# Attention moves shared between the GpSimd and SyncE queues in a fused attention and two-MLP kernel

## The chip, the cores and the metric

The kernel runs on one core of one Trainium2 chip. The metric is the device time of one execution in microseconds (us). Most executions of a kernel agree within 0.3%. The engines of the core are TensorE (PE in the profile, its weight loads PEld), VectorE (DVE), ScalarE (ACT), GpSimd (POOL) and SyncE (SP), which computes nothing and issues transfers. A name with a q (SPq, ACTq) is that engine's queue of issued instructions; transfers run on the core's 16 DMA engines.

## The reference

All tensors are float32. Attention has 4 batches, 12 heads, 448 rows and a head dimension of 64; the 12 heads' scores are mixed with one 12x12 matrix ahead of the softmax and with another behind it. Two MLPs follow, on 1792 tokens of 768 features.

```python
scores = scale * np.matmul(q, k.transpose(0, 1, 3, 2))
scores = np.einsum('bhij,hg->bgij', scores, w_pre)
scores = scores - np.max(scores, axis=-1, keepdims=True)
attn = np.exp(scores)
attn = attn / (np.sum(attn, axis=-1, keepdims=True) + 1e-09)
attn = np.einsum('bhij,hg->bgij', attn, w_post)
x = np.matmul(attn, v)            # -> [1792, 768], heads side by side
h = (x @ w1) * (x @ w2) @ w3 @ w_out
h = h @ w_in
out = np.maximum(0.01 * h, h) @ w_out2
```

## The kernel before, in words

The first 310 us or so are attention, the rest the MLPs. The change concerns attention alone, and there its beginning.

The 448 query rows of a batch are cut into four chunks (three of 120 rows, one of 88, which is computed with 90). The order of chunks (`order`) begins with the short one. A chunk consists of blocks of 10 query rows; two blocks are a group, and the program walks over groups two at a time (the loop over `k`, which grows by 2; each turn is called a step here, so k = 24 is the thirteenth step).

For a chunk, `qk` computes the scores of one head pair p in one go: two matmuls into PSUM (tile `pq`, for the even head e = 0 and the odd head e = 1), then a copy of each into SBUF (tile `s`, 120 rows x 2 heads x 448), by ScalarE or VectorE. The mixing over heads needs the heads of one query row on the partition axis. That is what `move` does: a DMA takes one head's 120 x 448 scores from tile `s` and writes them to ten partitions, twelve apart, of a row tile `sr`. A chunk has six pairs, so twelve moves. There are three row tiles (`rows_of`, numbered 0, 1, 2, each 128 x 12 x 448), used in turn; all three are cleared once at the beginning, in `constants_load`, since some partitions are never written.

`premix` multiplies a row tile with the pre-mixing matrix (`pm` in PSUM, from `sr` and `kpre` alone); `tops` takes row maxima on VectorE (`mx`); `softmax` exponentiates on ScalarE (tile `e`, sums in `sm`); `weigh` scales by the reciprocal of the sums, three of four tiles on GpSimd and the fourth on VectorE; `postmix` multiplies with the post-mixing matrix (`po`) on TensorE, and VectorE transposes the result (`ap`); `av` multiplies with v (`px`), and ScalarE writes `y`, with one subtraction on GpSimd. The first premix of a row tile needs all twelve moves of the chunk.

The work is issued in an order that is written out by hand (no scheduler moves it within attention). `qk` runs ahead: LEAD = 10 groups' pairs, eleven pairs in all, are computed before the first step with `early=True`, and each step then makes the pairs of two more groups (three at k = 16 and k = 20, by AT). In a step come: the `qk` matmuls, loads of q and k for later steps by SyncE, `tops`, `softmax`, `evict` (the copies of the new pairs and their moves), `av`, `weigh`, `postmix` of the step before, and the premixes of the next step. `turn(n)` are n matmuls without a result that fill time on TensorE.

The queues before: moves go by SyncE's queue, in the order in which the program reaches them, between the loads of q, k and v and the stores of y. Only the even heads of the first chunk go by ScalarE's queue. GpSimd's queue has no transfer in it. At the beginning VectorE clears row tile 0, and GpSimd clears `kpre`, `kpost` and row tiles 1 and 2. In the early `qk` VectorE copies the odd heads, and of the first chunk both heads of every second pair; ScalarE copies the rest.

Of the kernel before, what the change touches and what calls it, by code (L numbers as in the profile page):

```python
# [11 lines left out]
ACTF = mybir.ActivationFunctionType  # L12
# [10 lines left out]
def attention_moe_kernel(ctx: ExitStack, tc, qt, kt, vt, w_pre, w_post, w1, w2, w3t, w_out, w_in2, w_out2, out):  # L23
# [7 lines left out]
    nc = tc.nc  # L31
# [7 lines left out]
    P = 128  # L39
    JP = 112  # L40
    NJ = S // JP
    IB = 10
    LEAD, AT, SKIP = 10, (16, 20), 4
    CH = qt.shape[-1]
    TERMS = ((0, 0), (0, 1), (1, 0))
    scale = 1.0 / float(D) ** 0.5
# [71 lines left out]
    def attention(seam):  # L118
        with ExitStack() as es, ExitStack() as left:
# [30 lines left out]
            def constants_load():  # L150
                nc.vector.memset(rows_of[0], 0.0)
                for t in (kpre, kpost):
                    nc.gpsimd.memset(t, 0.0)
                for i in (1, 2):
                    nc.gpsimd.memset(rows_of[i], 0.0)
                for n, w in enumerate((w_pre, w_post)):
                    nc.sync.dma_start(out=wrep[:, n, :], in_=w)

# [68 lines left out]
            def qk(b, c, p, early=False):  # L227
# [28 lines left out]

                def out():
                    for e in range(2):
                        if early and (e or (b, c) == order[0] and p % 2):
                            nc.vector.tensor_copy(t[:m, e, :], pq[e][:m])  # L260
                        else:
                            nc.scalar.activation(out=t[:m, e, :], in_=pq[e][:m], func=ACTF.Copy)  # L262
                    for e in range(2):
                        args = srt[b, c], t[:m, e, :], 2 * p + e
                        move(*args, nc.sync if e or (b, c) != order[0] else nc.scalar)

                evs.append(out)
                if early:
# [4 lines left out]
                w = t.shape[0] // IB  # L273
                ends["sync"] = queue.dma_start(out=dst[SKIP + h:SKIP + h + H * (IB - 1) + 1:H, :w, :], in_=t)

            evs, staged = [], []

            def evict():
                while evs:
# [217 lines left out]
            for k in range(0, NG + 2, 2):  # L497
# [7 lines left out]
                old = [n for g in done for n in groups[g]]  # L505
                before = ets.pop(k - 2, None)
                ahead = [x for g in made[k] for x in slot(g)]
                for x in ahead:
                    qk(*x)
                for job in (k_load, q_load):  # L510
# [13 lines left out]
                if drain:  # L524
                    if old:
                        turns = postmix(old, before, now=False)
                        turn_out(turns.pop(0))
                    if k > LAST:
                        next(seam, None)
                    if now:  # L530
                        weigh(fresh, sm, ets[k], True)
                    while turns:
                        turn_out(turns.pop(0))
                else:
                    weigh(fresh, sm, ets[k], False)
                while lows:
                    lows.pop(0)()
                if old and not drain:
# [583 lines left out]
```

## Time and profile before

| | |
|---|---|
| three runs, us | 1218.69, 1223.53, 3006.95 (median 1223.53) |
| the profiled execution's own time, us | 1220.24 |
| its span in the profile, us | 1218.5 |
| granted TensorE clock, mean | 0.997 |
| busy: TensorE / weight loads | 98% / 81% |
| busy: VectorE / ScalarE / GpSimd | 73% / 45% / 17% |
| DMA, mean over the span | 162 GB/s |

The span is the time from the first to the last instruction of the profiled execution, and its own time is a little longer. Busy shares are means over stages with different limits: GpSimd is busy almost only in the first 310 us. Rows of the trace name a line of the kernel, the engine, the operation and the tiles (written <- read). A bracket at the end of a row of a timeline holds how long the engine was idle before it and what ended that idle time, by the profile's inference; a wait for several things is put down to the one that came last by it. A granted clock of 1.00 is 2.4 GHz, one of 0.50 is 1.2 GHz.

### The profile page before, as it was taken

The numbers are of one execution on the slowest core, as the hardware profiler recorded it, in microseconds if no ns is written. First come the engines' busy times: TensorE is split into PE (matmuls) and PEld (weight loads), VectorE is DVE, ScalarE is ACT, GpSimd is POOL, SyncE is SP. The second block draws the span as 40 slices with busy tenths as digits, with TensorE's granted clock in tenths as the row PEclk, the third lists the DMA queues.
The fourth block names the chain that finished last, engine by engine and source line by source line (L and its number), as shares of the span: only waits on it lengthen the run. The fifth ranks groups of instructions, "written<-read, shape, count | busy, mean of one in ns | idle before, by whom it ended". The sixth has DMA issues, their size and how long they took to land.

```text
span 1218.5 us, 22377 instructions
## 1 busy us (share of the span) xinstructions
PE 1197.1 (98%) x8782; PEld 985.3 (81%) x8782; DVE 885.8 (73%) x1538; ACT 550.8 (45%) x1120; POOL 206.8 (17%) x160
## 2 busy tenths in 40 slices
PE   8899999999999999999999999999999999999998
PEld 5245555554478999998899999999999999999998
DVE  6677887888889998547795867667776657376572
ACT  3677777766755454323454342352233433322120
POOL 4566767666310000000000000000000000000000
PEclk9999999999999999999999999999999999999999
DMA  6876776756957756489674636063242221212012
GB/s 212 222 201 192 211 231 183 221 168 184 300 160 256 238 187 198 162 275 352 221 238 145 216 96 208 26 221 115 92 129 70 65 70 52 72 33 72 26 53 91
DMA packets 134282, 196.81 MB, mean 162 GB/s; under 512 B 26304, under 2 KB 114976, under 8 KB 134176
## 3 DMA queue, kind: packets, MB, share of 16 engines
q1 hardware_dynamic: 129656, 192.77, 49.7%
q10 hardware_dynamic: 4520, 2.61, 0.7%
q8 instruction: 69, 1.13, 0.4%
q14 instruction: 37, 0.30, 0.1%
HBM read 114.57 MB, written 42.07 MB: 129 GB/s over the span
## 4 chain that ended last, share of the span: by engine, by line
PE 82%; DVE 8%; DMA 5%; ACT 3%; issue 1%; ACTq 0%; SPq 0%; POOL 0%; DVEq 0%; POOLq 0%
PE pm L587 29%; PE po L601 19%; PE pp L898 17%; DVE ap L375 6%; PE pw L659 6%; PE px L392 5%; PE po L360 3%; ACT e L323 3%; DMA sr<-s 3%; PE pq L248 2%; DVE mx L316 1%; DMA x<-scr 1%; PE pm L306 1%; DMA q<-in_q_dram 1%; PE turn L293 1%
## 5 line engine op out<-in xcount | busy, mean ns | idle before, releaser
L587 PE MATMUL pm<-x,ws 128*128 128x384 f32 (+1 forms) x1152 | 233.9, 364 | 0.0
L587 PEld LDWEIGHTS pm<-x,ws 128*128 128x128 f32 x1152 | 208.7, 188 | 24.5 <-issue 0.6
L339 POOL TENSOR_SCALAR e<-e,sm 128x448 f32<-128x448 f32 x126 | 181.9, 1456 | 141.0 <-DVE sm L333 123.1
L323 ACT ACTIVATE e<-pm,mx 128x448 f32<-128x448 f32 x180 | 111.7, 632 | 85.3 <-DVE mx L316 80.8
L375 DVE STREAM_TRANSPOSE ap<-po 128x512 f32<-128x512 f32 (+3 forms) x228 | 116.7, 571 | 25.2 <-PE po L360 24.5
L898 PE MATMUL pp<-t,w 128*128 128x448 f32 x576 | 124.5, 368 | 0.0
L601 PE MATMUL po<-ws,g 128*128 128x384 f32 x672 | 117.2, 334 | 0.0
L601 PE MATMUL po<-wo,g 128*128 128x384 f32 x672 | 117.1, 334 | 0.0
L898 PEld LDWEIGHTS pp<-t,w 128*128 128x128 f32 x576 | 108.1, 188 | 10.9
L601 PEld LDWEIGHTS po<-wo,g 128*128 128x128 f32 x672 | 116.6, 188 | 0.2
L601 PEld LDWEIGHTS po<-ws,g 128*128 128x128 f32 x672 | 116.6, 188 | 0.0
L316 DVE TENSOR_REDUCE mx<-pm 128x1 f32<-128x448 f32 x180 | 98.5, 603 | 11.7 <-PE pm L306 11.7
L100 ACT ACTIVATE wc<-wr 128x768 f32<-128x768 f32 (+1 forms) x72 | 61.6, 858 | 85.0 <-DMA wr<-in_moe_w_dram 29.1
L392 PEld LDWEIGHTS px<-ap,vs 96*64 96x64 f32 (+1 forms) x1536 | 77.7, 136 | 22.1 <-ACT e L323 16.7
L898 PE MATMUL pp<-b,w 128*128 128x448 f32 x432 | 95.5, 368 | 0.0
L608 DVE TENSOR_TENSOR acc<-po,acc 128x384 f32<-128x384 f32 x84 | 45.5, 555 | 66.5 <-PE po L601 66.4
L306 PE MATMUL pm<-sr,kpre 64*64 64x448 f32 x720 | 82.0, 555 | 9.0 <-DMA sr<-s 4.8
L392 PE MATMUL px<-ap,vs 96*64 96x120 f32 (+3 forms) x1536 | 87.6, 266 | 2.9 <-ACT e L323 1.0
L360 PE MATMUL po<-e,kpost 64*32 64x512 f32 (+1 forms) x1472 | 89.1, 586 | 0.8 <-POOL e L339 0.7
L262 ACT ACTIVATE s<-pq 120x448 f32<-120x448 f32 (+1 forms) x178 | 82.2, 563 | 12.7 <-PE pq L248 10.9
L898 PEld LDWEIGHTS pp<-b,w 128*128 128x128 f32 x432 | 81.1, 188 | 8.0
L248 PEld LDWEIGHTS pq<-k,q 64*120 64x120 f32 (+1 forms) x528 | 44.6, 176 | 46.9 <-DVE ap L375 17.6
(104 smaller groups left out, 1580.9 us busy)
## 6 DMA issues: line engine op xcount, KB each, us to landing
sr<-s SPq DMA_DIRECT2D x144, 210.0 KB
wr<-in_moe_w_out_dram SPq DMA_DIRECT2D x24, 768.0 KB
wr<-in_moe_w_dram SPq DMA_DIRECT2D x16, 768.0 KB
wr<-in_moe_w_in_dram SPq DMA_DIRECT2D x16, 768.0 KB
wr<-in_moe_w_dram SPq DMA_DIRECT2D x16, 512.0 KB
sr<-s SPq DMA_DIRECT2D x42, 157.5 KB
vs<-in_v_dram SPq DMA_DIRECT2D x12, 512.0 KB
kept_w<-wc SPq DMA_DIRECT2D x16, 384.0 KB
```

The source lines that it names most:

```text
L262: nc.scalar.activation(out=t[:m, e, :], in_=pq[e][:m], func=ACTF.Copy)
L306: nc.tensor.matmul(pms[ns[s % len(ns)]][half:half + Q], kpre[rows], sr[rows, 2 * t + g, :], start=True, stop=True,)
L316: nc.vector.tensor_reduce(out=mxs[n], in_=pms[n], axis=AX.X, op=ALU.max, negate=True)
L323: ends["act"] = nc.scalar.activation(out=e[:, i], in_=pms.pop(n), func=ACTF.Exp, bias=mxs.pop(n), scale=1.0, accum_out=sm[:, i:i + 1])
L339: ends["dve" if eng is nc.vector else "pool"] = eng.tensor_scalar(out=e[:, i], in0=e[:, i], scalar1=rc[:, i:i + 1], scalar2=None, op0=ALU.mult
L360: nc.tensor.matmul(po[g][32 * r:32 * (r + 1), :m], kpost[rows, x], e[rows, :m, JS[r]:JS[r] + P], start=True, stop=True,)
L375: ends["dve"] = nc.vector.transpose(out=dst, in_=po[g][:, i0:i1])
L392: nc.tensor.matmul(px[e * D:(e + 1) * D, r, :nw].rearrange("p (n i) -> p n i", i=HQ), vs[rows, p, jc, e, :], ap[rows, x, :ns, jc, h * HQ:( ...
L587: nc.tensor.matmul(dst, wt[:, a, kk, :], x[kk][:, c, c0:c0 + w], start=(i == 0), stop=(i == len(steps) - 1))
L601: nc.tensor.matmul(po, g[m][:, a, t * P:(t + 1) * P], wts[m][:, c, cs], start=(m == 0 and j == 0), stop=(m == FQ - 1 and j == 2),)
L659: nc.tensor.matmul(pw, wt[:, x, kk, :], wos[kk][y][:, cs], start=(kk == 0 and j == 0), stop=(kk == KF - 1 and j == 2),)
L898: nc.tensor.matmul(dst, w[:, i, a, kk, :], b[:, kk, c, :], start=(kk == 0 and j == 0), stop=(kk == KH - 1 and j == 2),)
```

## The change

Four things change.

1. In the early `qk`, ScalarE copies every even head and VectorE every odd head, in the first chunk too.
2. The moves of the early even heads go by GpSimd's queue, of all early chunks; ScalarE's queue issues none any more. The early odd heads stay with SyncE.
3. In the steps up to k = 22 (`SOFT` = 24, twelve steps) the moves of even heads are kept in a list `soon` and issued on GpSimd's queue behind `weigh` of the same step; the odd ones go by SyncE at the old place. From k = 24 on all go by SyncE as before.
4. Row tile 2 is cleared by ScalarE, as a copy of the cleared tile `kpre` spread over it, no longer by GpSimd.

```diff
-    LEAD, AT, SKIP = 10, (16, 20), 4
+    LEAD, AT, SOFT, SKIP = 10, (16, 20), 24, 4
...
-                for i in (1, 2):
-                    nc.gpsimd.memset(rows_of[i], 0.0)
+                nc.gpsimd.memset(rows_of[1], 0.0)
+                none = rows_of[2].rearrange("p n s -> p (n s)").rearrange("p (a b) -> p a b", b=Q)
+                nc.scalar.activation(
+                    out=none, in_=kpre.unsqueeze(1).to_broadcast([P, CH // IB * S // Q, Q]), func=ACTF.Copy
+                )
...
                     for e in range(2):
-                        if early and (e or (b, c) == order[0] and p % 2):
+                        if early and e:
                             nc.vector.tensor_copy(t[:m, e, :], pq[e][:m])
                         else:
                             nc.scalar.activation(out=t[:m, e, :], in_=pq[e][:m], func=ACTF.Copy)
                     for e in range(2):
                         args = srt[b, c], t[:m, e, :], 2 * p + e
-                        move(*args, nc.sync if e or (b, c) != order[0] else nc.scalar)
+                        if early or e or not soft[0]:
+                            move(*args, nc.sync if e or not early else nc.gpsimd)
+                        else:
+                            soon.append(args)
...
-            evs, staged = [], []
+            evs, staged, soon, soft = [], [], [], [True]
...
+                soft[0] = k < SOFT
                 for x in ahead:
                     qk(*x)
...
                     weigh(fresh, sm, ets[k], False)
+                    while soon:
+                        move(*soon.pop(0), nc.gpsimd)
```

How instructions stand on the engines, in program order. In these rows sr_108, sr_106 and sr_107 are row tiles 0, 1 and 2, and "x6" is six of the same in a row.

GpSimd, from the clearings to the first weighings; before:

```order
L153 MEMSET kpre 128x64
L153 MEMSET kpost 128x64
L155 MEMSET sr_106 128x5376
L155 MEMSET sr_107 128x5376
L339 TENSOR_SCALAR e<-e,sm 128x448 x15
L405 TENSOR_TENSOR y<-y 128x2x88
```

The same place now:

```order
L153 MEMSET kpre 128x64
L153 MEMSET kpost 128x64
L154 MEMSET sr_106 128x5376
L280 DMA sr_108<-s 10x9x448 x6
L280 DMA sr_106<-s 10x12x448 x5
L345 TENSOR_SCALAR e<-e,sm 128x448 x3
L280 DMA sr_106<-s 10x12x448
L280 DMA sr_107<-s 10x12x448
L345 TENSOR_SCALAR e<-e,sm 128x448 x3
L280 DMA sr_107<-s 10x12x448 x2
```

One clearing has gone, eleven early moves stand ahead of the first weighings, and two (in two steps three) behind the three weighings of each step: 26 in the twelve steps, 37 with the early ones.

ScalarE, from its start to the first exponentials; before:

```order
L262 ACT_TABLE_LOAD
L262 ACTIVATE s<-pq 90x448
L274 DMA sr_108<-s 10x9x448 x2
L262 ACTIVATE s<-pq 90x448
L274 DMA sr_108<-s 10x9x448 x2
L262 ACTIVATE s<-pq 90x448
L274 DMA sr_108<-s 10x9x448 x2
L262 ACTIVATE s<-pq 120x448 x5
L323 ACTIVATE e,sm<-pm,mx 128x448 x4
```

The same place now:

```order
L156 ACT_TABLE_LOAD
L156 ACTIVATE sr_107<-kpre 128x5376
L265 ACTIVATE s<-pq 90x448 x6
L265 ACTIVATE s<-pq 120x448 x5
L329 ACTIVATE e,sm<-pm,mx 128x448 x4
```

The six moves have gone, three copies (VectorE's before) have come, and the clearing of row tile 2 stands ahead of all. TensorE's order is the same as before. SyncE has the same loads and stores in the same order, with half as many moves between them up to the twelfth step: its first run of moves is six of row tile 0 and one of row tile 1, where it was six and two, and then come the two q loads.

## Rows read from the trace of the kernel before

**Rows 1.** The page's first line: the span.

```profile
span 1218.5 us, 22377 instructions
```

**Rows 2.** Windows: stretch, length, each engine's busy us, granted clock, DMA share, GB/s.

```profile
core 0: us, PE busy (x) PEld busy (x) DVE busy (x) ACT busy (x) POOL busy (x), PEclk, DMA share, GB/s
...
0.00:90.00 90.00, 77.77 (x750) 38.61 (x750) 61.25 (x128) 51.25 (x134) 50.40 (x41) 0.96 0.74 212
...
90.00:1218.50 1128.50, 1119.33 (x8040) 946.65 (x8032) 824.58 (x1411) 499.56 (x986) 156.38 (x120) 1.00 0.49 158
...
12.00:19.00 7.00, 6.30 (x38) 3.31 (x34) 6.08 (x18) 2.83 (x6) 0.00 (x0) 1.00 0.62 204
...
130.00:135.00 5.00, 4.93 (x78) 2.73 (x80) 3.43 (x8) 4.64 (x15) 3.03 (x4) 1.00 1.09 277
37.50:41.00 3.50, 3.50 (x12) 1.13 (x8) 1.50 (x4) 2.21 (x6) 0.38 (x1) 0.51 0.99 223
81.90:85.30 3.40, 3.39 (x16) 1.84 (x18) 1.60 (x3) 1.74 (x7) 0.87 (x2) 0.50 0.81 243
```

**Rows 3.** Timeline of TensorE: start, length, what [idle before, what ended it].

```profile
16.57 1.02 PE L248 MATMUL pq<-k,q 64*120 64x448 f32 x4 [0.69 <-ACT s L262]
17.52 1.60 PE L293 MATMUL turn<-spare 128*128 128x128 f32 x12
21.32 1.73 PE L306 MATMUL pm<-sr,kpre 64*64 64x448 f32 x16 [2.19 <-DMA sr<-s]
...
25.03 1.02 PE L248 MATMUL pq<-k,q 64*120 64x448 f32 x4 [1.03 <-DMA q<-in_q_dram]
...
36.81 1.15 PE L306 MATMUL pm<-sr,kpre 64*64 64x448 f32 x8 [2.57 <-DMA sr<-s]
...
59.04 1.09 PE L306 MATMUL pm<-sr,kpre 64*64 64x448 f32 x8 [2.21 <-DMA vs<-in_v_dram]
...
81.91 1.88 PE L306 MATMUL pm<-sr,kpre 64*64 64x448 f32 x8 [2.00 <-DMA q<-in_q_dram]
```

**Rows 4.** Chain that ended last: start, length, what.

```profile
31.27 5.45 DMA sr<-s
...
54.77 12.33 DMA sr<-s
```

**Rows 5.** Moves by issuing queue, whole program: ns min/median/max, first and last start.

```profile
L274 SPq DMA_DIRECT2D sr<-s x186: 755/756/1527, 8.6 to 313.0; - x186
...
L274 ACTq DMA_DIRECT2D sr<-s x6: 785/794/1414, 8.5 to 14.5; - x6
```

**Rows 6.** Timeline of GpSimd: clearings, weighings of five steps, a subtraction.

```profile
1.40 9.10 POOL L155 MEMSET sr<- 128x5376 f32 x2
26.15 4.34 POOL L339 TENSOR_SCALAR e<-e,sm 128x448 f32<-128x448 f32 x3 [15.66 <-ACT s L262]
32.79 4.35 POOL L339 TENSOR_SCALAR e<-e,sm 128x448 f32<-128x448 f32 x3 [2.29 <-ACT s L262]
...
48.62 4.40 POOL L339 TENSOR_SCALAR e<-e,sm 128x448 f32<-128x448 f32 x3 [3.84 <-DVE sm L333]
...
70.76 4.34 POOL L339 TENSOR_SCALAR e<-e,sm 128x448 f32<-128x448 f32 x3 [2.79 <-DVE sm L333]
75.08 0.55 POOL L405 TENSOR_TENSOR y<-y 128x176 fp32r<-128x176 f32 x1
77.77 4.34 POOL L339 TENSOR_SCALAR e<-e,sm 128x448 f32<-128x448 f32 x3 [2.13 <-DVE sm L333]
...
103.10 4.34 POOL L339 TENSOR_SCALAR e<-e,sm 128x448 f32<-128x448 f32 x3 [2.22 <-DVE sm L333]
...
111.49 4.36 POOL L339 TENSOR_SCALAR e<-e,sm 128x448 f32<-128x448 f32 x3 [3.38 <-DVE sm L333]
```

**Rows 7.** ScalarE: its first copy (timeline); its widest copies (lines by form).

```profile
7.88 0.54 ACT L262 ACTIVATE s<-pq 90x448 f32<-90x448 f32 x1 [5.88 <-PE pq L248]
...
L72 ACT ACTIVATE w<-w 128x1536 fp32r<-128x1536 f32 x8 | 11.9, 1486 | 7.0 <-DMA w<-sums_w 7.0
```

**Rows 8.** Timeline of VectorE: its share of the first step's weighing.

```profile
26.01 0.45 DVE L339 TENSOR_SCALAR e<-e,sm 128x448 f32<-128x448 f32 x1
```

## The prediction

> **What bounds the kernel now.** I read the windows first [rows 2]. From 90 us to the end TensorE is busy for 1119.33 of 1128.50 us, so whatever is saved or lost ahead of 90 us should reach the end nearly one to one. From 0 to 90 us it is busy for 77.77 of 90.00 us: 12.2 us of idle time. The change acts there and up to about 120 us, so that idle time, and two short stretches at the lower clock, are all that it can win.
>
> Then TensorE's own order of time [rows 3]. Four times it stands before a premix (pm): 2.19 us at 21.32, 2.57 us at 36.81, 2.21 us at 59.04 and 2.00 us at 81.91. The page puts the first two down to the landing of a move (sr<-s), the others to a v and a q load; but a premix reads only sr and kpre, and all four are the first premix of a row tile, which needs all twelve moves of that tile. I read all four as moves that landed late. Two smaller waits belong to them: 0.69 us for a ScalarE copy at 16.57, and 1.03 us for a q load at 25.03 that SyncE issued behind eight moves. Behind the second and the fourth wait the granted clock is 0.51 and 0.50, the lower level, for 3.5 and 3.4 us [rows 2]; each such stretch costs about half of itself, 1.7 us.
>
> Why are the moves late? The chain of waits has a move that took 5.45 us from issue to landing, and 20 us later one that took 12.33 us [rows 4]. SyncE needs only about 0.76 us for one [rows 5]. Between 12 and 19 us, when moves are all that is under way, the DMA engines run at a share of 0.62 and 204 GB/s; between 130 and 135 us, with loads and stores beside them, at full share and 277 GB/s [rows 2]. 0.62 is ten of sixteen, and a move writes ten partitions: I read this as moves that keep ten engines full while six stand idle, and so as a backlog that feeds on itself, with both the issuing queue and these ten engines as limits.
>
> **The change part by part.**
>
> *Which engine copies and issues at the beginning.* ScalarE loses its six moves (0.79 us each, median [rows 5]), which stood between its copies, and copies six even heads of the first row tile instead of three. Three copies more and six moves fewer are a gain for it. VectorE has three copies fewer. So the 0.69 us wait for a ScalarE copy goes. The pairs of premixes can then begin when the fillers of 1.60 us behind that pq are done, at 17.52 - 0.69 + 1.60 = 18.4, say 18.5 instead of 21.32, if the moves have landed.
>
> *The clearing.* ScalarE clears 5376 columns. Its nearest row does 1536 in 1.486 us [rows 7], so at most 5.2 us by proportion. The engine's first copy came at 7.88, after 5.88 us of idle time: the clearing fits into it, and costs nothing. GpSimd's two clearings took 9.10 us from 1.40; with one it is free at 6.0, ahead of the first move at about 8.45.
>
> *The price of a move on GpSimd.* The trace shows none. Below, GpSimd could hand it on at once (0); above, the longest issue by a SyncE queue is 1.527 us, and its median 0.756 [rows 5]. A software-run engine is likelier above that median than below: I take c = 1.0 us, between them. Issue to landing has 5.45 us in a backlog as the upper end and, as the lower one, a move's 215 KB at 204 GB/s, 1.05 us, plus an issue of 0.76, so 1.8. Half the moves leave SyncE's queue but the loads stay, so I take 4.4 us, nearer the upper end, with c within it.
>
> *First row tile.* GpSimd issues six moves from 8.42 (7.88 + 0.54) on; back to back the last starts at 13.4, with a gap for a copy at 13.9. Landing 13.9 + 4.4 = 18.3, ahead of 18.5. Gain 21.32 - 18.5 = **2.8 us**. With 5.45 us it lands at 19.4 and the gain is 1.9.
>
> *Second tile.* Its last even head is copied in the first step and now stands behind GpSimd's three weighings, which end at 26.15 + 4.34 = 30.5 [rows 6], in times of before. Landing 30.5 + 4.4 = 34.9 instead of 36.81: **1.9 us**, the q wait included. With 1.8 us all 3.6 would go, with 5.45 us 0.9.
>
> *Third tile.* The weighings end at 48.62 + 4.40 = 53.0; landing 57.4 instead of 59.04: **1.6 us** (2.2 at best, 0.6 with 5.45).
>
> *Fourth tile.* The weighings end at 70.76 + 4.34 = 75.1; landing 79.5, ahead of 79.9 where TensorE began to wait: **2.0 us** (1.4 with 5.45).
>
> *The clock.* Without the fourth wait the stretch behind it should stay at the upper level: 1.7 us. Behind the second some wait is left, so I count half of it: 0.85. Together **2.5 us**, bounds 0 and 3.4.
>
> *What is late next.* GpSimd's round. In the first steps it is three weighings and two moves, 4.34 + 2.0 = 6.35 us; the step took 6.64 (26.15 to 32.79), and 5.6 without the q wait. I charge 0.7 us for two such steps, **1.4 us**. Later steps add a subtraction of 0.55 us (it starts at 75.08): 4.9 + 2.0 = 6.9 against a step of 7.01 (70.76 to 77.77); a step with three moves needs 8.0 and took 8.39 (103.10 to 111.49). So c = 1.0 just fits, and nothing is charged. Behind a late weighing stand the postmix (po) on TensorE, then VectorE's transposes.
>
> *A rule against it.* VectorE's scaling of a weight tile takes 0.45 us at 26.01 [rows 8], just as GpSimd's own weighing starts, so it ends 4 us before GpSimd's next move: by these rows the two don't meet, and the charge is nothing. The Trainium skill ("SBUF — State Buffer", section "SBUF: two separate sides") says that GpSimd cannot write the descriptors of its DMAs while VectorE runs an operation that uses the port both share. By that rule twelve such meetings would cost at most 12 x 0.45 = 5.4 us, an estimate, and the sum would be about 1216; no run here shows it yet.
>
> **The sum.** 2.8 + 1.9 + 1.6 + 2.0 + 2.5 = 10.8 saved, 1.4 charged: 9.4 us. The profiled execution took 1220.24 us for a span of 1218.5 [rows 1], so 1210.8, **1211 us**. The median of the three runs is 1223.53, with 1218.69 below it; the profiled time lies between them.
>
> **The rivals.**
>
> *A. The ten engines stay the limit.* If GpSimd's moves fill the same ten engines, half the queue moves and the backlog stays. For it: SyncE's 0.76 us per move is below the 1.05 us of transfer, so transfer is the tighter limit. Against it: part of the waits comes from order (the q load behind eight moves, the ScalarE copy behind moves). It would save these, 0.69 + 1.03 us, and perhaps 1.5 us at the first tile, and pay 1.4: about 1218. The Trainium skill ("DMA: Bandwidth & Descriptors", section "Issuing engines are not separate DMA queues") says that DMAs from all engines run on the same sixteen DMA engines, so that spreading them saves issue time alone; the share of 0.62 is what leaves room for more here.
>
> *B. GpSimd becomes the bound (slower).* Its round is full at c = 1.0. With c = 2.0 the first four steps need 8.35 us against about 6.3 (+8), six steps with two moves 8.9 against 7.0 (+11.5), two with three 10.9 against 8.4 (+5): 24.5. The first tile's last move starts at 18.4 and lands near 23.8, a loss of 2.5 instead of a gain of 2.8. Of the 10.8 some 5 are left at the other tiles and the clock at most, and slack between weighing and postmix swallows about 4 once: +18, about 1238. At c = 3.0 it is 26 us more, about 1264. The gains are used up near c = 1.5. For it: nothing in the trace prices a move on GpSimd. Against it: 0.8 us on the other two queues.
>
> *C. More is saved.* Landing in about 3 us and c near the queues' 0.8: the first tile 2.8, then 3.4, 2.2 and 2.0, the clock 3.4, charge about 0.5: 13.3 us, 1207.
>
> **How the numbers follow.** The forecast, 1209 to 1215: 0.45. C, 1204 to 1209: 0.17. A, 1215 to 1220: 0.20. B: 0.18, of which 0.08 up to 1226, 0.05 up to 1245 and 0.05 above. The range 1204 to 1226 leaves out 0.10 above and some 0.03 below. 2%, about what a measurement of this kernel can tell from no change, is 24.5 us: faster would need more than all the idle time of the first 90 us, 0.01; slower needs c above 2.3, 0.05; within 2%, 0.94.
>
> **What would show it.** Right: TensorE's first premix near 18.5 us; each of the four waits under 1.6 us; no or one stretch at half clock before 90 us; a landing in the chain well under 12 us; moves of about 1 us on GpSimd's queue. Wrong: GpSimd's weighing starting later behind VectorE's reciprocal, with postmixes waiting for it (B); four waits as before with a share near 0.65 (A). The forecast falls if moves on GpSimd cost more than 1.5 us, or if a wait saved early is met again at a later load.

## The result and the profile after

| | before | after |
|---|---|---|
| median of 9 runs each, us | 1219.60 | 1227.77 |
| profiled execution: its time, its span, us | 1220.24, 1218.5 | 1227.77, 1226.0 |
| mean granted clock | 0.997 | 0.993 |

The changed kernel is slower: the ratio of its time to that of before is 1.0064, with a 95% interval of 1.004 to 1.0088, so 4.9 to 10.7 us of 1219.6. The forecast was 1211 us with a range of 1204 to 1226. Both the sign and the size were missed.

The windows of the changed kernel's trace, with the columns of [rows 2]; the first two answer to its first two:

```profile
0.00:90.00 90.00, 72.35 (x667) 34.91 (x668) 57.45 (x118) 52.61 (x124) 57.06 (x61) 0.92 0.75 199
90.00:1226.00 1136.00, 1126.83 (x8120) 951.43 (x8114) 828.06 (x1417) 505.35 (x1001) 168.18 (x136) 1.00 0.50 157
12.00:19.00 7.00, 5.43 (x34) 3.07 (x30) 4.64 (x15) 3.26 (x6) 4.19 (x8) 1.00 0.85 197
22.30:29.10 6.80, 3.77 (x18) 1.36 (x20) 1.64 (x3) 1.32 (x4) 0.00 (x0) 0.50 0.71 202
63.30:70.10 6.80, 6.26 (x32) 2.76 (x34) 3.31 (x7) 3.19 (x8) 1.39 (x1) 0.50 0.69 180
90.60:94.00 3.40, 3.40 (x18) 2.50 (x18) 2.66 (x6) 2.98 (x8) 2.41 (x4) 0.50 1.03 282
```

From 90 us on TensorE is idle for 1136.00 - 1126.83 = 9.17 us, the same 9.17 us as before (1128.50 - 1119.33). The whole difference of 7.5 us in span is made by about 94 us. Up to 90 us the idle time grew from 12.2 to 17.7 us, and up to 94 us two long stretches and a shorter one run at half clock, where before there were two short ones [rows 2].

TensorE's timeline of after at the first premix of each of the four row tiles (start, length, what, and in brackets the idle time before it and what ended it):

```profile
25.32 3.26 PE L312 MATMUL pm<-sr,kpre 64*64 64x448 f32 x16 [7.89 <-DMA q<-in_q_dram]
...
39.72 0.98 PE L312 MATMUL pm<-sr,kpre 64*64 64x448 f32 x8 [0.94 <-issue]
...
63.84 1.88 PE L312 MATMUL pm<-sr,kpre 64*64 64x448 f32 x8 [5.36 <-DMA k<-in_k_dram]
...
89.35 1.19 PE L312 MATMUL pm<-sr,kpre 64*64 64x448 f32 x8 [1.77 <-DMA sr<-s]
```

Against [rows 3] the four premixes start 4.0, 2.9, 4.8 and 7.4 us later, and the 7.4 us last to the end. As before, a premix reads sr and kpre alone, so the loads named in two brackets are only the last event that the profile could put there. I read the waits as moves that landed late. Where the trace has the landing of a tile's last even move, it fits at the second tile (35.52 + 3.8 = 39.3), the third and the fourth; at the first it does not suffice, which is taken up further below.

The moves of after by queue over the whole program (ns min/median/max, first and last start), and under them the time from issue to landing of those on GpSimd's queue:

```profile
L280 SPq DMA_DIRECT2D sr<-s x155: 755/756/2217, 7.8 to 320.3; - x155
L280 POOL DMA_DIRECT2D sr<-s x37: 580/595/777, 8.0 to 124.0; - x37
...
DMA to landing us min/median/max: 2.8/5.9/11.7
```

A move costs GpSimd 0.6 us, less than SyncE's 0.76 us [rows 5]. But it lands 5.9 us after its issue in the median, and at the longest 11.7 us. GpSimd's own timeline shows where they are issued: five for the second tile at 14.11 to 17.35 us, and from then on two behind each three weighings.

```profile
14.11 1.74 POOL L280 DMA_DIRECT2D sr<-s  x3 [0.51 <-issue]
...
16.77 0.58 POOL L280 DMA_DIRECT2D sr<-s  x1 [0.17 <-issue]
31.23 4.34 POOL L345 TENSOR_SCALAR e<-e,sm 128x448 f32<-128x448 f32 x3 [13.88 <-ACT s L265]
35.52 1.20 POOL L280 DMA_DIRECT2D sr<-s  x2
...
54.19 1.21 POOL L280 DMA_DIRECT2D sr<-s  x2
```

Of the two moves of a step the first completes a tile in the steps that start these waits: that at 35.52 the second tile, that at 54.19 the third. The landing of the two at 54.19 and 54.8 us (the first of them took 9.5 us):

```profile
DMA to landing us min/median/max: 9.5/9.8/10.1
```

54.19 + 9.5 = 63.7, and the third premix starts at 63.84.

When had the kernel before issued the same moves? SyncE's timeline of before, at the steps that complete the second, the third and the fourth tile:

```profile
28.66 7.32 SPq L274 DMA_DIRECT2D sr<-s  x8
...
48.42 3.80 SPq L274 DMA_DIRECT2D sr<-s  x4
...
70.73 4.42 SPq L274 DMA_DIRECT2D sr<-s  x4
```

The first move of each row is the tile's last even head, issued 6.9, 5.8 and 12.0 us earlier than in after (35.52, 54.19, 82.75). From there to the premixes of before at 36.81, 59.04 and 81.91 are 8.2, 10.6 and 11.2 us.

The chain of after that ended last (start, length, what), where [rows 4] had a 5.45 us and a 12.33 us move:

```profile
20.96 4.37 DMA q<-in_q_dram
...
52.61 11.16 DMA k<-in_k_dram
...
80.02 2.73 POOL e L345 x2
82.75 5.93 DMA sr<-s
```

At the fourth tile the chain goes through GpSimd: its weighing ends at 82.75, only then is the move issued, and it takes 5.93 us. At the third the chain names a k load that SyncE issued at 52.61, ahead of GpSimd's moves at 54.19 us.

Last, what the transfers did from 10 to 22 us, when nearly all of them are moves. First before, then after: bytes and rate, then each queue's packets, MB and the share of 16 engines that its packets took.

```profile
DMA packets 1521, 2.44 MB, mean 204 GB/s; under 512 B 142, under 2 KB 1521, under 8 KB 1521
...
q1 hardware_dynamic: 921, 1.47, 40.1%
q10 hardware_dynamic: 600, 0.97, 24.5%
```

```profile
DMA packets 1091, 2.31 MB, mean 193 GB/s; under 512 B 331, under 2 KB 825, under 8 KB 1091
...
q0 software_dynamic: 548, 1.43, 56.3%
q1 hardware_dynamic: 543, 0.88, 28.0%
```

Before, 64.6% of 16 engines for 12 us is 124 us of engine time for 2.44 MB, 51 us for a MB. After, GpSimd's queue (q0) takes 56.3%, 108 us for 1.43 MB, 76 us for a MB, and SyncE's (q1) 54 us for 0.88 MB, 61 us for a MB. The engines are busy for 84% instead of 65% of the time, and they move 5% less in a second. The early part of what follows turns on this pair of rows.

### The profile page after: what moved, and what is told of

Its sections match the earlier page's. It is cut to its first block, busy times and chain, and to the rows that moved or that the text cites. A ratio compares the mean times of both kernels' runs of the same rounds, so it can differ in the third digit from the quotient of the medians.

```text
span 1226.0 us, 22402 instructions
## 1 busy us (share of the span) xinstructions
PE 1199.2 (98%) x8782; PEld 986.3 (80%) x8782; DVE 885.5 (72%) x1535; ACT 558.0 (46%) x1124; POOL 225.2 (18%) x196
## 4 chain that ended last, share of the span: by engine, by line
PE 83%; DVE 8%; ACT 4%; DMA 3%; issue 1%; SPq 1%; POOL 1%; ACTq 0%; DVEq 0%; POOLq 0%
PE pm L596 29%; PE po L610 19%; PE pp L907 17%; DVE ap L381 6%; PE pw L668 6%; PE px L398 5%; PE po L366 3%; ACT e L329 3%; PE pq L251 2%; PE pm L312 1%; DVE mx L322 1%; DMA x<-scr 1%; DMA k<-in_k_dram 1%; PE turn L299 1%; POOL e L345 1%
## 5 line engine op out<-in xcount | busy, mean ns | idle before, releaser
L312 PEld LDWEIGHTS pm<-sr,kpre 64*64 64x64 f32 x720 | 25.0, 134 | 73.8 <-issue 31.0
```

What stands on the lines that cost most here:

```text
L312: nc.tensor.matmul(pms[ns[s % len(ns)]][half:half + Q], kpre[rows], sr[rows, 2 * t + g, :], start=True, stop=True,)
```

## The experiments

The change has two parts: the early moves (first two row tiles, ahead of the steps), and the moves of the steps. Two causes were weighed for the first part and two for the second: that the second tile's moves take transfer time from the first tile's last ones, or that moves on GpSimd's queue are slow in themselves; and that an even move is late because it now stands behind the loads that SyncE issues in the step, or because it is on GpSimd and its weighing. Ratios are to the kernel before on the same chip, with 95% intervals; each kernel has 10 runs, the one with SyncE behind the loads 5. The edits are against the changed kernel, unless another is named.

### The early part alone

```diff
-    LEAD, AT, SOFT, SKIP = 10, (16, 20), 24, 4
+    LEAD, AT, SOFT, SKIP = 10, (16, 20), 0, 4
```

> The change ahead of the first step alone: in the steps even heads go by SyncE's queue at the old place again (SOFT = 0). Theory O: the first premix still starts near 25.3 us, 4 us late; the third and the fourth tile wait as before the change or less, so about 3 to 4 us above the kernel before. If all of the loss came from the steps (the moves that stand behind the weighings), it would be at the time of the kernel before or under it.

Measured: 1221.77 us, ratio 1.0018 [0.9992, 1.0044]. TensorE's timeline at the first tile, and then at the second, where there is no wait at all:

```profile
26.34 3.14 PE L312 MATMUL pm<-sr,kpre 64*64 64x448 f32 x16 [8.86 <-DMA sr<-s]
...
38.72 1.72 PE L312 MATMUL pm<-sr,kpre 64*64 64x448 f32 x12
```

The late first premix is the early part's doing: 5.0 us later than before. Little of it lasts, since the second tile is then complete when it is wanted: the third tile's premix starts at 59.22 us, where before it started at 59.04. The interval holds 1, so over its runs this kernel can't be told from before.

### The moves of the steps alone

The early part, its copies and its clearing as before (those hunks are left out here); the steps as in the change.

```diff
-                            move(*args, nc.sync if e or not early else nc.gpsimd)
+                            move(*args, nc.sync if e or (b, c) != order[0] else nc.scalar)
```

> The change in the steps alone: the early copies, the early moves and the clearing are as before, and only the even heads of the twelve steps go by GpSimd's queue behind the weighings. Theory W (an even head's move that waits for three weighings lands late for the third and the fourth tile): first premix at 21.3 us as before, a wait of about 4 to 5 us ahead of the third tile's first premix, the whole 3 to 4 us above the kernel before. If the early part alone costs, this one is at the time of the kernel before within 1 us or below it.

Measured: 1225.92 us, ratio 1.0036 [1.0016, 1.0056]. The timeline at the third and the fourth tile, and under it the two even moves of the step that completes the third tile, the first its last, the second the fourth tile's first (ns of one issue, first and last start; then us to landing):

```profile
63.94 1.88 PE L309 MATMUL pm<-sr,kpre 64*64 64x448 f32 x8 [7.08 <-DMA sr<-s]
...
88.66 1.09 PE L309 MATMUL pm<-sr,kpre 64*64 64x448 f32 x8 [1.50 <-issue]
```

```profile
L277 POOL DMA_DIRECT2D sr<-s x2: 582/604/627, 53.0 to 53.6; - x2
...
DMA to landing us min/median/max: 10.3/10.3/10.4
```

53.0 + 10.3 = 63.3, 0.6 us ahead of the third premix: but for these 0.6 us the even move accounts for the wait. The larger half of the loss is in the steps. With 0.18% for the early part the two make 0.54%, which is within the interval of the whole change (0.40 to 0.88%).

### Early: only the first tile's even heads on GpSimd

```diff
-                            move(*args, nc.sync if e or not early else nc.gpsimd)
+                            move(*args, nc.sync if e or (b, c) != order[0] else nc.gpsimd)
```

With the moves of the steps as in the change:

> The change, but of the early even heads only those of the first row tile go by GpSimd's queue; the five of the second tile go by SyncE's, behind the first tile's. The steps are as in the change. Theory O (overtaking: the DMA engines give out about 200 GB/s of moves whichever queue they come from, and the second tile's moves on GpSimd's queue were served ahead of the first tile's last ones on SyncE's): the first premix starts near 20.5 us instead of 25.32, the low clock behind it goes, and the whole is 5 to 6 us below the change. Rival S (moves by GpSimd's queue are slow in themselves, their packets taking longer per byte): the six that remain still hold the first tile up, first premix near 23 us or later, at most 2 us gained. Rival C (ScalarE's clearing or its copies are late): first premix stays near 25 us.

Measured: 1224.99 us, ratio 1.0051 [1.0026, 1.0076]. And with the steps as before:

```diff
-    LEAD, AT, SOFT, SKIP = 10, (16, 20), 24, 4
+    LEAD, AT, SOFT, SKIP = 10, (16, 20), 0, 4
-                            move(*args, nc.sync if e or not early else nc.gpsimd)
+                            move(*args, nc.sync if e or (b, c) != order[0] else nc.gpsimd)
```

> GpSimd's queue for the first tile's six even heads alone; everything else goes by SyncE's queue in the old order (the first experiment's early part and SOFT = 0 together). Theory O and W together: first premix near 20.5 us or a little earlier, the later waits as before, so 0 to 2 us below the kernel before. Rival S: about 2 us above it.

Measured: 1219.65 us, ratio 0.9991 [0.9965, 1.0017]. The first premixes, of the one and of the other:

```profile
23.10 3.27 PE L312 MATMUL pm<-sr,kpre 64*64 64x448 f32 x16 [4.86 <-DMA q<-in_q_dram]
```

```profile
22.94 3.05 PE L312 MATMUL pm<-sr,kpre 64*64 64x448 f32 x16 [5.55 <-DMA q<-in_q_dram]
```

Taking only the second tile's five early moves off GpSimd's queue brings the first premix 2.2 us forward with the steps (25.32 to 23.10) and 3.4 us without (26.34 to 22.94). So moves of the second tile did delay the first tile. About 2 us remain that the first tile's own moves on GpSimd cost; the 20.5 us of theory O were not met in either kernel, nor were the 2 us of time that rival S wrote down for the second. The two kernels differ in nothing but the steps, and in time by about 0.6%: the steps cost most of what the change costs.

### Early: all even heads on ScalarE

Against the early part alone; the copies and the clearing stay as in the change.

```diff
-                            move(*args, nc.sync if e or not early else nc.gpsimd)
+                            move(*args, nc.sync if e or not early else nc.scalar)
```

> The change ahead of the first step alone, but all eleven early even heads go by ScalarE's queue where the change has GpSimd's; copies and clearing as in the change, steps as before it. Theory O (overtaking between two queues): the second tile's five even moves are again issued ahead of the first tile's last odd ones in the DMA engines, and the first premix comes at 23 us or later. Rival S (GpSimd's queue is slow in itself): the first premix comes at 20 to 21.5 us.

Measured: 1219.06 us, ratio 1.0003 [0.998, 1.0026]. The same with the second tile's even heads on SyncE, so that only the copies and the clearing differ from before:

```diff
-                            move(*args, nc.sync if e or not early else nc.gpsimd)
+                            move(*args, nc.sync if e or (b, c) != order[0] else nc.scalar)
```

> The early copies and the clearing of the change, with the first tile's six even heads on ScalarE's queue and all the rest on SyncE's: against the run with these six on GpSimd's queue, only that queue differs. Rival S (GpSimd's moves take longer in the DMA engines): the first premix comes at 20 to 21.3 us instead of 22.9, and the time is 0 to 2 us below the kernel before. If it comes near 23 us, the new copies or the clearing, not the queue, hold the first tile up.

Measured: 1218.38 us, ratio 1.0001 [0.9979, 1.0023]. First premixes:

```profile
20.93 1.91 PE L312 MATMUL pm<-sr,kpre 64*64 64x448 f32 x16 [1.29 <-DMA sr<-s]
```

```profile
20.20 1.74 PE L312 MATMUL pm<-sr,kpre 64*64 64x448 f32 x16 [0.48 <-DMA sr<-s]
```

The second kernel and the one with the first tile's moves alone on GpSimd differ in that queue only: 20.20 against 22.94 us, in profiles of the shortest of its ten runs and of the longest of the other's; the spread over all kernels stands further below. So two queues by themselves do not delay the first tile, and neither do the new copies or ScalarE's clearing; GpSimd's queue does. The first kernel does not show whether early moves of the second tile on ScalarE's queue would delay it as well: the issuing holds up ScalarE's copies, and the five start at 16.6 to 24.6 us, where GpSimd's started at 14.1 to 16.8. The second kernel had the shortest span of all profiled here, 1212.1 us, but over its runs it is equal to before.

### Early: only the second tile's even heads on GpSimd

Against the early part alone:

```diff
-                            move(*args, nc.sync if e or not early else nc.gpsimd)
+                            move(*args, nc.sync if e or not early else nc.scalar if (b, c) == order[0] else nc.gpsimd)
```

> The early part of the change, steps as in before, but the first row tile's even heads go by ScalarE's queue (as in before) and only the second tile's early even heads by GpSimd's. Overtaking (the second tile's moves, sent off early by an idle queue, take transfer time from the first tile's last moves): the first premix starts at 24 us or later, with a wait of 5 us or more, though no move of the first tile is on GpSimd's queue; the second premix tile is early. Slow queue (what goes by GpSimd's queue lands late in itself): the first premix starts at 20 to 21.5 us as with ScalarE's queue alone (wait of 0.5 to 2.2 us), and the second tile's part is later than 37 us. Total by overtaking about 1221 us, by the slow queue about 1219 us.

Measured: 1220.02 us, ratio 0.9996 [0.9973, 1.0019]. The first premix, and GpSimd's moves of the first 22 us:

```profile
21.96 3.26 PE L312 MATMUL pm<-sr,kpre 64*64 64x448 f32 x16 [2.80 <-DMA q<-in_q_dram]
```

```profile
L280 POOL DMA_DIRECT2D sr<-s x5: 580/582/776, 17.3 to 19.8; - x5
```

Neither number that was written down was met: 21.96 lies between the 24 us of the one and the 21.5 us of the other. The reason can be read from the second row: with ScalarE issuing again, the copies come later, and GpSimd's five moves start at 17.3 instead of 14.1 us. The run took the early start away along with the queue, so it tells the two causes apart only weakly: 1.0 us later than with all even heads on ScalarE's queue, and 1.8 us later than with the second tile's on SyncE's (20.20), the kernel that differs from it in these five moves alone.

### Early: the first tile alone on the way

The even heads of the first tile on GpSimd, the steps as before, and the second tile's early moves held back. Against the early part alone:

```diff
+                        if early and (b, c) != order[0]:
+                            soon.append(args)
-                        if early or e or not soft[0]:
-                            move(*args, nc.sync if e or not early else nc.gpsimd)
+                        elif early or e or not soft[0]:
+                            move(*args, nc.sync if e or (b, c) != order[0] else nc.gpsimd)
...
             premix(1)
+            while soon:
+                move(*soon.pop(0), nc.sync)
```

> The first row tile's even heads by GpSimd's queue, the second tile's ten early moves all held back and sent by SyncE after the first premixes have been issued, steps as in before. Overtaking: with nothing of the second tile in the way the first premix starts at 18.5 to 20 us, below all kernels so far, and the second tile's premix is later (37 us or more). Slow queue: the first premix starts at 22 to 23 us as in the kernel with the first tile's moves alone on GpSimd's queue (22.94). Total 1219 to 1222 us by either.

Measured: 1219.58 us, ratio 1.0004 [0.9984, 1.0024]. The first premix, and the transfers from 10 to 22 us:

```profile
22.41 2.65 PE L314 MATMUL pm<-sr,kpre 64*64 64x448 f32 x16 [4.61 <-DMA sr<-s]
```

```profile
DMA packets 1231, 2.24 MB, mean 186 GB/s; under 512 B 271, under 2 KB 1065, under 8 KB 1231
...
q1 hardware_dynamic: 880, 1.34, 43.5%
q0 software_dynamic: 351, 0.89, 28.0%
```

The first tile is still not complete before 22.41. The way was not wholly free: SyncE does not wait for the premix, so it sent its q loads from 15.65 us on and the second tile's moves from 19.65. But until then nothing of the second tile was asked for, and the tile's last even move, issued at 13.4, took 8.2 us to land. That is the slow queue: from 10 to 22 us the transfers run at 186 GB/s where before they ran at 204. Both queues take 60 to 62 us of engine time for a MB (28.0% of 192 us for 0.89 MB, 43.5% for 1.34 MB), against 51 before, so SyncE's transfers get slower too when GpSimd's run beside them.

For the first tile both causes are thus real: 22.41 to 23.10 us in three kernels with its even heads on GpSimd and the second tile's not, against 20.20 to 21.32 in the seven whose early part has no move on GpSimd (before, the two with ScalarE, the four with the early part as before), some 2 us for the queue; and another 2.2 to 3.4 us for the second tile's moves issued from 14.1 us on. The landings say how. In the three kernels the last even move lands at 21.6 to 21.9 us, and the premix follows 0.8 to 1.4 us later. With the second tile's moves on GpSimd as well it lands at 21.0 (after) and 23.5 (the early part alone), and TensorE waits another 4.3 and 2.9 us. Then only SyncE's odd moves can be missing, whose landings the traces do not show. None of this is seen in the time: the six kernels with the steps as before all have intervals that hold 1.

### Steps: GpSimd's moves ahead of its weighing

Against the moves of the steps alone:

```diff
                 evict()
+                while soon:
+                    move(*soon.pop(0), nc.gpsimd)
...
                     weigh(fresh, sm, ets[k], False)
-                    while soon:
-                        move(*soon.pop(0), nc.gpsimd)
```

> The change in the steps alone, as in the experiment on the steps, but GpSimd issues the even heads' moves ahead of its three weighings, right behind the copies. Early part as before the change. Theory W (the place behind the weighings: in that time SyncE has put a v and a k load into the DMA engines, and the third tile's last even move queues behind them): the third tile's wait falls from 7.1 us to about that of the kernel before, 2 to 3 us, and the time to within 2 us of the kernel before. Rival S (a move by GpSimd's queue is slow wherever it stands): that wait stays at 5 us or more, and the time 4 us or more above.

Measured: 1221.84 us, ratio 1.0023 [1.0004, 1.0042]. The third premix, of TensorE's waits from 14 to 100 us that for GpSimd (total, times, longest), and the landing of the two even moves of the step that completes the third tile:

```profile
62.78 1.09 PE L309 MATMUL pm<-sr,kpre 64*64 64x448 f32 x8 [2.14 <-DMA sr<-s]
```

```profile
PE po L363 <- POOL e L342: 2.4, 3, 1.8
...
DMA to landing us min/median/max: 9.0/9.2/9.3
```

The third tile's wait goes back to 2.1 us, about that of before, but not because the tile is complete much earlier: its premix starts only 1.2 us earlier than in the steps alone (62.78 for 63.94). TensorE comes to it 3.8 us later, since postmixes now wait for the weighing that stands behind the moves, and since the second tile's wait has grown to 4.13 us (2.57 before). And the third tile's last even move, issued at 52.1 us and so ahead of that step's v load at 53.9, still took 9.0 us to land. The loads that theory W puts ahead of it are therefore not the whole of its lateness.

### Steps: SyncE's queue, behind the loads

Against the moves of the steps alone: no move of a step on GpSimd; SyncE issues the even ones behind the step's v load and the next k and q loads.

```diff
                 for job in (k_load, q_load):
                     do(k // 2, job)
+                while soon:
+                    move(*soon.pop(0), nc.sync)
...
                     weigh(fresh, sm, ets[k], False)
-                    while soon:
-                        move(*soon.pop(0), nc.gpsimd)
```

> No move by GpSimd at all. The even heads of the twelve steps go by SyncE's queue, but behind the v, k and q loads that SyncE issues next, which is where GpSimd's moves of the change come in time. Early part as before the change. Theory W (late place): the wait ahead of the third tile's first premix is 4 us or more though the queue is SyncE's, and the time is 2 to 6 us above the kernel before. Rival S (GpSimd's queue itself): the third tile waits 2 to 3 us as in the kernel before, and the time is that of the kernel before within 1 us.

Measured: 1224.14 us, ratio 1.004 [1.0006, 1.0075]. The third premix:

```profile
62.75 1.09 PE L309 MATMUL pm<-sr,kpre 64*64 64x448 f32 x8 [4.06 <-DMA sr<-s]
```

Without any move of the steps on GpSimd the loss is still there, in the time as in the wait. A late place on SyncE's own queue is enough.

### Steps: the v loads behind the moves

Against the moves of the steps alone:

```diff
                     while soon:
                         move(*soon.pop(0), nc.gpsimd)
+                    if 0 < k <= NPAIR:
+                        v_load(0, k // 2 - 1, nc.gpsimd)
...
-                if 0 < k <= NPAIR:
-                    v_load(0, k // 2 - 1)
```

> The change of the steps alone (early part as in before), and the first eight v loads are asked for by GpSimd right behind its even-head moves instead of by SyncE ahead of them. Place (the even move lands late since the step's v, k and q loads were put ahead of it): with the v loads behind the move, the third tile's wait falls from the 7.1 us of the steps-alone kernel to 2 to 4 us and the time to 1220 to 1222 us. Queue (the move is late because GpSimd's queue is slow or because the weighing ends late): the wait stays at 5 us or more and the time at 1224 to 1226 us.

Measured: 1222.58 us, ratio 1.0026 [1.0008, 1.0044]. The third and the fourth premix, and the two even moves of the step that completes the third tile, its last the first of them:

```profile
61.57 1.09 PE L309 MATMUL pm<-sr,kpre 64*64 64x448 f32 x8 [3.10 <-ACT e L326]
...
83.92 1.10 PE L309 MATMUL pm<-sr,kpre 64*64 64x448 f32 x8 [1.49 <-issue]
```

```profile
L277 POOL DMA_DIRECT2D sr<-s x2: 587/620/653, 54.5 to 55.2; - x2
...
DMA to landing us min/median/max: 6.6/6.8/6.9
```

54.5 + 6.9 = 61.4, just ahead of the premix at 61.57: here the even move lands when the premix starts, whatever the bracket names. Issued 1.5 us later than with the v loads ahead, it lands 3.4 us sooner after its issue (6.9 for 10.3), and the premix starts 2.4 us earlier. The wait falls by more, from 7.08 to 3.10 us, as the place predicts, but 1.6 us of that is TensorE's coming later. The fourth premix comes 4.7 us earlier (83.92 for 88.66), though the moves are still GpSimd's and still behind its weighing. The time, 1222.58, ends just above the 1220 to 1222 us written down.

What stays open in the steps: the four variants (the steps alone, ahead of the weighing, SyncE behind the loads, v loads behind) lie at 1.0036, 1.0023, 1.004 and 1.0026 with intervals of about 0.002 to each side, so how the loss divides between the place, the queue and the delayed weighing is not settled by these times. That a late place alone suffices, and that GpSimd's moves ahead of the weighing still cost something, is: both intervals lie above 1. Single profiles must be read with care here: with the steps as before the third tile's wait was between 0.33 us (the early part alone) and 5.85 us (all early even heads on ScalarE). The start of its premix tells more than the wait: 61.57 to 63.94 us in the six kernels with the steps changed, 55.30 to 60.34 in six with the steps as before; the seventh of these, with the first tile's moves alone on GpSimd, has 64.12, in a profile of the longest of its ten runs (1225.1 us).

No kernel tried is faster than before. The times part in two: the six with the steps as before have ratios of 0.9991 to 1.0018, and every interval holds 1; the six with the moves of the steps changed, the whole change among them, have 1.0023 to 1.0064, and every interval lies above 1. The loss that the times show is made in the steps.

## Why the prediction was wrong, point by point

**What bounds the kernel.** Right in that the difference is made by about 94 us, up to the fourth tile's first premix and the low clock behind it, and that what is left there reaches the end undiminished. But within that time gains and losses at the four tiles do not simply add up, as the sum had them: of the 5.0 us lost at the first tile in the early part alone 0.2 us were left at the third, since the waits in between took them up.

**The landing, 4.4 us: the step that failed.** The prediction took a time from issue to landing between 1.8 and 5.45 us and added it to the issue of the last even move, at each of the four tiles. The first tile's even moves were issued when it said (the last at 13.01 us, forecast 13.9 at the latest), yet the tile was complete at 25.32, not at 18.3. Its last even move landed at 13.01 + 8.0 = 21.0, and the rest was SyncE's. The moves on GpSimd's queue from 13.0 us on, the first tile's last (8.0 us) and the second's five (10.1 to 11.7), with their time from issue to landing below:

```profile
L280 POOL DMA_DIRECT2D sr<-s x6: 580/580/596, 13.0 to 16.8; - x6
...
DMA to landing us min/median/max: 8.0/10.3/11.7
```

The landing was treated as a property of a move. In these traces it goes with all that is asked for at the time: the rate stayed near 200 GB/s from 12 to 19 us, and what the second tile asked for sooner made the first tile's rest wait. The trace of before spoke against 4.4 us too. By the prediction's own reading of the four waits, the time from the issue of a tile's last even head to the premix was 6.8 us at the first tile (14.5 [rows 5] to 21.32) and 8.2, 10.6 and 11.2 us at the others, above the 5.45 us of its upper end each time. The prediction set the new issue against the old premix and never asked when the old kernel had issued the same move; behind the weighings it is issued 5.8 to 12.0 us later, delay carried along from the tile before included. The prediction counted the second tile's five moves on GpSimd's queue at no price for the first, although a queue with no copies and no loads in it must issue them earlier. And it followed only the even moves; SyncE's odd ones are needed just as much.

**Where it failed, tile by tile.** First tile: +2.8 forecast, -4.0 measured. Second: from the issue at 35.52 to the premix at 39.72 are 4.2 us, so here the 4.4 us were right, but the weighing ended 5 us later than in before (35.6 for 30.5). Third: 54.19 to 63.84, 9.6 us instead of 4.4, about what it had been before (10.6), from a later issue. Fourth: 5.93 us in the chain, behind a weighing that ended at 82.75, where the same step's ended at 70.76 + 4.34 = 75.1 before [rows 6]: by then what was lost at the third tile had moved the weighing itself. The prediction did see that even moves now stand behind the three weighings; it did not see that in the same step they stand behind SyncE's loads as well. How much of the lateness in the steps is the later issue, the loads ahead, GpSimd's queue or the delayed weighing stays open.

**The clock.** +2.5 us forecast. Instead TensorE was busy for 3.77 + 6.26 + 3.40 = 13.4 us at half clock against 6.9 before. At half lost in each, 6.7 us against 3.4: -3.3. The idle time before the four premixes, with the two small waits of before, rose from 10.7 to 16.0 us. 5.3 and 3.3 are 8.6 us, close to the 7.4 us by which the fourth premix is late.

**The price on GpSimd.** c = 1.0 us forecast, 0.595 measured, below the 0.76 and 0.79 us of the other two queues, and rival B's 18 us did not come. The charge of 1.4 us for GpSimd's round did not show either: no matmul of a postmix waits for GpSimd's weighing, and its weight loads do so three times, for 2.0 us in all. B's bound was not far, though: in six of the first nine steps GpSimd is idle for only 0.4 to 1.2 us ahead of a weighing.

**Copies and clearing.** Right. ScalarE's timeline of after:

```profile
2.02 4.68 ACT L156 ACTIVATE sr<-kpre 128x5376 f32<-128x5376 f32 x1
7.15 0.54 ACT L265 ACTIVATE s<-pq 90x448 f32<-90x448 f32 x1 [0.45 <-PE pq L251]
```

The clearing takes 4.68 us (bound: 5.2), the first copy starts at 7.15 instead of 7.88, and the 0.69 us wait for a copy is gone. With the queues left alone this is worth nothing that the runs can tell: 1.0001.

**The share of 0.62.** The prediction read it as ten engines full and six idle, with room to win. The room was not there. From 12 to 19 us the share rose from 0.62 to 0.85 and the rate fell from 204 to 197 GB/s. Rival A had this half right, that the transfers stay the limit; it expected only a gain that fails to come, 1218 us, not that the moves would get slower (186 to 194 GB/s from 10 to 22 us in the five kernels with the first tile's even heads on GpSimd, among them after; 203 to 212 in before and the three with them on ScalarE and the new copies). The rule that it cited, from the Trainium skill ("DMA: Bandwidth & Descriptors", section "Issuing engines are not separate DMA queues"), says that spreading the issue over engines adds no transfer engines; the 204 and 197 GB/s agree with it.

**VectorE and the port.** GpSimd's 37 issues take 0.580 to 0.777 us, also those that lie beside VectorE's copies at 14 to 17 us, so no issue was lengthened by a VectorE operation of 0.45 us. In the steps VectorE's scaling of a weight tile ended some 4 us before the moves, as the prediction had it. The rule from the Trainium skill ("SBUF — State Buffer", section "SBUF: two separate sides"), priced at up to 5.4 us, shows in none of these rows; whether descriptors were written late once an issue had ended, they can't tell.

**The chances.** C (1207) needed landings of 3 us. B's range up to 1226 nearly reached the time, for another reason. The parts add up to 1.00 without the 0.03 that it leaves below 1204. There was no case for moves that land later than 5.45 us, although [rows 4] had one of 12.33 us in plain sight. That row should have been the upper end of the landing.

## What to carry to other kernels

Where several queues feed the same transfers, a time to landing read from one queue does not hold on another: sum what all queues will have asked for by then, at the rate that the stretch has shown, and ask which requests the freed queue will now send earlier. Take the time to landing from the very move that is to be moved, from its issue in the old kernel to the work that waits for it. A DMA share below 1 is no spare rate until a row shows more GB/s at a higher share for the same kind of transfer; the 277 GB/s of [rows 2] were loads and stores beside moves. And a transfer moved to another engine's queue is taken out of an order: look at what stands ahead of it there, and also at what the old queue now sends first.

## What the runs showed of the hardware

A move issued by GpSimd costs that engine 0.58 to 0.78 us (median 0.595), less than on SyncE (median 0.756). Its packets are larger, 2.6 KB on average against 1.6 KB (1.43 MB in 548, 2.44 MB in 1521), but the engine time for a MB goes up, on GpSimd's queue and on SyncE's beside it: 51 us with the hardware queues alone, 58 to 65 us on both queues in the three kernels with six moves of the first tile on GpSimd, and 76 us on GpSimd's queue (61 on SyncE's) with the second tile's five as well, 72 and 64 in the early part alone. With those five alone on GpSimd it is, again from 10 to 22 us, 83 us on GpSimd's queue, but still 51 on SyncE's and ScalarE's. The rate stays between 186 and 212 GB/s from 10 to 22 us all the while, at shares from 0.65 to 0.84. What it is that holds these moves there was not tried.
